# A retention block with a multiplicative FFN on one core: state products, weight conversion and copies in the head of the kernel put in another order

## The chip, the cores and the metric

The kernel runs on one core of a Trainium2 chip, with nothing on the other cores. The metric is the time of one execution on the device in microseconds (us), as the median over several executions. A core has five engines that work side by side, each with its own list of instructions which it takes strictly in order: TensorE (PE in the profile; its weight loads are shown apart as PEld), VectorE (DVE), ScalarE (ACT), GpSimd (POOL) and SyncE (SP), which here only issues transfers. An instruction waits until the engines and transfers it depends on have signalled.

## The reference, cut to what matters

```python
def _attn_ref(q, k, v):                      # 8 batches, 8 heads, 576 positions, 64 wide
    scores = scale * np.matmul(q, k.transpose(0, 1, 3, 2))
    gamma = 1.0 - 2.0 ** (-5.0 - np.arange(H))
    Dmat = np.where(rel >= 0, gamma[:, None, None] ** rel[None, :, :], 0.0)
    return np.matmul(scores * Dmat[None], v)

def _moe_ref(x, w1, w2, w3, w_out):          # x: 4608 tokens x 512
    a = x @ w1                               # 512 x 1024
    b = x @ w2
    h = a * b @ w3                           # 1024 x 1024
    return h @ w_out                         # 1024 x 512

# reference: x = attention out, (B,H,S,D) -> (B*S, H*D); out = _moe_ref(x, ...)
```

q, k and v are float32. The four weights are float64, and the kernel turns them into float32 itself, from their two 32-bit halves.

## The kernel before

**Attention by units.** The causal decay is split between the queries and the keys (the latter by scaling v), so that a sequence can be worked off in chunks with a running state. A unit `g` is a pair of batches and one of five chunks of positions (64, 128, 128, 128, 128). Unit `g` needs: its transfers (`load`); the scaling of q and of v by decay factors (`scale`, on GpSimd, VectorE or ScalarE as the call says); `front`, which transposes k and q on TensorE and copies them out of PSUM on ScalarE; `score`, the products of k and q on TensorE, masked by VectorE into `pm`; `state`, which adds k times v onto the running state in PSUM and copies it to `sb` for the next unit (ScalarE); and `pv`. `pv(g)` makes the unit's output in two PSUM banks: first the product of q with the state of the units before (L305, nothing for the first chunk), then `pm` times v (L312), and then ScalarE copies the banks into the token tiles `xT` (L317). Of the seven PSUM banks of the pool `acc`, all these products and those of the FFN take one each in turn.

**FFN by Strassen's scheme.** x @ w1 and x @ w2 are made with seven products in place of eight (`up(i, n, fp)`: 192 tokens of each of two batches, quarter `fp` of the columns). `up` needs sums of weights (`strassen_weights`, four VectorE operations L171, of which S2 is the second) and sums of tokens (`strassen_tokens`, L499). Its products follow each other on TensorE (L527): p1 (A11 B11), S2 T2, S3 T3, S1 T1, A22 T4, A12 B21, S4 B22. VectorE takes them into the tile `c` with adds (L532), ScalarE with copies (L540, L555), and L561 multiplies the two halves. S4 B22 is added onto the bank of S1 T1, and so waits for that product's add. w3 and w_out are multiplied with each other first (`w3_mm`), and the result is used in `down`.

**Weight conversion.** The weights come in blocks of 128 x 512 float64 (`load_block`, five raw buffers, so block n+5 can be loaded once block n is read). Blocks 0 to 3 are the first quarter of w1 and w2, 4 to 7 the second quarter, and so on. A block is converted by

- `begin_block`: three ScalarE steps for the exponent (L398 takes the top 16 bits without the sign, L399 turns them into the exponent's complement, L400 into the bits of a float), beside VectorE's L402 (top mantissa bits) and L405 (lower half added);
- `end_block`: VectorE's L416 (sign) and L429 (mantissa times power of two, into the weight tile). Behind that the next block to load is issued on SyncE's queue, and after the last block of a quarter come the four weight sums.

Both are written as a generator, `conversion()`, which stops after each step: L402 with the ScalarE steps is one, L405 one, L416 one, L429 one, the weight sums three. `convert(n)` runs the next n steps at the place where it is called, and `convert_up_to(n)` runs until n blocks are done. The list of numbers in L450 says behind how many converted blocks the next one is not begun ahead; otherwise a block is begun before the one in front of it is ended. `up` calls `convert` after each add (argument `conv`) and once after its first product, with a count taken from the list `owed`.

**The order.** No scheduler reorders: `manual_schedule` keeps every engine's list in the order of the program. The head of the kernel, L693 to L774, is written out by hand: units 0 to 4 with their transfers on SyncE's queue, the conversions between them, and the first five `up` calls. From L776 on loops take over.

Names used below: "unit 1" is the second unit (`g = 1`), "block 7" the eighth block. In the profile, `ld_q`, `ld_v` are the raw tiles, `tp` transposes, `kT`, `qT` their copies, `sc` scores, `st` the state in PSUM, `xps` the two output banks, `e` and `m` exponent and mantissa of a block, `wA` converted weights, `wS` weight sums, `T` token sums.

Of the kernel before, what the change touches and what calls it, by code (L numbers as in the profile page):

```python
# [42 lines left out]
def kernel(  # L43
# [202 lines left out]
    def score(g):  # L246
        c = g % NC
        sz = sizes[c]
        kT, qT = live["kT", g], live["qT", g]
        pm = pools["fr"].tile([P, 2, 2, NP, P], F32, tag="pm", name="pm", bufs=1)  # L250
        for b in range(2):
            sc = [acc.tile([P, NP, P], F32, tag="acc", name="sc") for j in range(2)]
            for p in range(NP):
                for j, hs in enumerate(heads):
                    nc.tensor.matmul(sc[j][:sz, p, :sz], kT[hs, b, p, :sz], qT[hs, b, p, :sz],  # L255
                                     start=True, stop=True)
            for j in range(2):
                nc.vector.tensor_mul(pm[:sz, b, j, :, :sz], sc[j][:sz, :, :sz],  # L258
                                     mask[:sz, :sz].unsqueeze(1).to_broadcast([sz, NP, sz]))
        live["pm", g] = pm  # L260

    def state(g):
        c = g % NC
        sz = sizes[c]
        if c == NC - 1:
            return
        vs = live["v", g]
        kn = live["k", g]
        if c == 0:
            live["st"] = st_ps.tile([P, 2, NP, D], F32, tag="st", name="st")  # L270
        st = live["st"]

        for b in range(2):
            for p in range(NP):
                for j, hs in enumerate(heads):
                    h = b * H + 2 * p + j
                    nc.tensor.matmul(st[hs, b, p, :], kn[:sz, h, :], vs[:sz, h, :],  # L277
                                     start=(c == 0 and b == 0 and p == 0), stop=(c == NC - 2),
                                     skip_group_check=True)
        sb = pools["fr"].tile([P, 2, NP, D], F32, tag="sb", name="sb")  # L280
        nc.scalar.copy(sb, st)
        live["sb", g + 1] = sb

    def pv(g):
        i, c = divmod(g, NC)
        sz = sizes[c]
        live["x", g] = True
        qT, vs, pm = live["qT", g], live["v", g], live["pm", g]

        parts = []  # L290
        for n in range(NB):
            lo, hi = max(starts[c], n * TB), min(starts[c] + sz, (n + 1) * TB)
            if lo < hi:
                m = i * NB + n
                if ("xT", m) not in live:
                    live["xT", m] = xps[m % 4 == 3].tile([P, NP, 2, TB], F32, tag="xT", name="xT")
                parts.append((live["xT", m], lo - n * TB, lo - starts[c], hi - lo))

        banks = [acc.tile([P, 2, 2, P], F32, tag="acc", name="xps") for r in range(2)]
        order = [(b, n) for b in range(2) for n in range(2)]  # L300
        if c > 0:
            for m, (b, n) in enumerate(order):
                for r, j in ((0, 0), (0, 1), (1, 0), (1, 1)):
                    p = 2 * r + n
                    nc.tensor.matmul(banks[r][heads[j ^ r], b, n, :sz], live["sb", g][heads[j], b, p, :],  # L305
                                     qT[heads[j], b, p, :sz], start=(m == 0), stop=False,
                                     skip_group_check=True)
        for m, (b, n) in enumerate(order):
            for r in range(2):
                for half in range(2):  # L310
                    p, j = 2 * r + n, half ^ r
                    nc.tensor.matmul(banks[r][heads[half], b, n, :sz], vs[:sz, b * H + 2 * p + j, :],  # L312
                                     pm[:sz, b, j, p, :sz], start=(c == 0 and m == 0), stop=True,
                                     skip_group_check=True)
        for x, to, fr, n in parts:
            for r in range(2):
                nc.scalar.copy(  # L317
                    x[:, 2 * r:2 * r + 2, :, to:to + n].rearrange("p n b s -> p b n s"),
                    banks[r][:, :, :, fr:fr + n])

# [60 lines left out]
    def begin_block():  # L383
        n = begun[0]
        t = live["raw", n]
        lo, hi = t[:, :, 0], t[:, :, 1]
        top = t.rearrange("p n t -> p (n t)").bitcast(BF16).rearrange("p (n u) -> p n u", u=4)[:, :, 3]
        e = raw.tile([P, CV], I32, tag="exp", name="e")
        m = raw.tile([P, CV], I32, tag="man", name="m")
        vec = nc.vector  # L390

        half = e.bitcast(BF16).rearrange("p (n u) -> p n u", u=2)[:, :, 1]
        func = mybir.ActivationFunctionType
        nc.scalar.activation(half, top, func.Abs)  # L398
        nc.scalar.activation(e, half.bitcast(U16), func.Relu, bias=lim[:, 0:1], scale=-1.0 / 16.0)  # L399
        nc.scalar.activation(e, e, func.Relu, bias=lim[:, 1:2], scale=-2.0 ** 23)  # L400

        vec.tensor_scalar(out=m, in0=hi, scalar1=0x000FFFFF, scalar2=0x00100000,  # L402
                          op0=ALU.bitwise_and, op1=ALU.bitwise_or)
        yield
        vec.scalar_tensor_tensor(m.bitcast(F32), in0=lo.bitcast(U32), scalar=2.0 ** -32, in1=m,  # L405
                                 op0=ALU.mult, op1=ALU.add)
        live["em", n] = e, m
        begun[0] += 1
        yield
# [34 lines left out]
    def conversion():  # L444

        yield from begin_block()
        while converted[0] < len(blocks):
            if begun[0] < len(blocks) and converted[0] not in (1, 2, 3, 7):  # L450
                yield from begin_block()
            yield from end_block()
            if begun[0] == converted[0] < len(blocks):
                yield from begin_block()
# [17 lines left out]
    def convert_up_to(n):  # L472
        while converted[0] < n:
            assert go_on() is None
# [231 lines left out]
    scale(0, "v")  # L706
    state(0)
    convert_up_to(1)
    pv(0)
    load(2, "kqv")  # L710
    load_block()
    load_block()
# [6 lines left out]
    convert(2)  # L719
    scale(1, "v")  # L720
    score(1)
    state(1)
    load(3, "kq")
    convert_up_to(3)
    convert(2)
    weight_sums = strassen_weights(0)
    next(weight_sums)
    pv(1)
    keep_busy(4)
    load(3, "v")  # L730
    load_block()
# [10 lines left out]
    convert(1)  # L742
    score(2)
    state(2)
    front(3, "k")
    scale(3, "q", True)
    load(4, "kq")
    convert(1)
    scale(3, "v", engine=nc.vector)
    convert(2)  # L750
    pv(2)
    front(3, "q")
    convert(2)
    load(4, "v")
    state(3)
    while ("S", 1) not in live:
# [3 lines left out]
    up(0, 0, 1, conv=2, tail=False)  # L760
    owed.append(2)
    front(4)
    pv(3)
    list(strassen_tokens(0, 1, nc.vector))
    score(4)
    aside.append(lambda: scale(4, "v", True))
    up(0, 1, 0, conv=2, tail=False)
    owed.append(2)
    pv(4)
    up(0, 1, 1, conv=[2, 1, 0, 2, 2], tail=False)  # L770
    owed.append(2)
    up(0, 0, 2, conv=[2, 1, 1, 2, 2], tail=False)
    owed.append(2)
    att_part.close()  # L774


# [92 lines left out]
    for g in range(NC, G):  # L869
        c = g % NC  # L870

        n = (1, 1, 1, 3, 1)[c] if g < 2 * NC else -(-len(todo) // (NC - c))
        if g + 2 < G and not in_blocks[g + 2]:
            load(g + 2, "k")
            load_blocks(g + 2, "q")
        if g + 1 < G:
            scale(g + 1, "v")
            if not in_blocks[g + 1]:
                front(g + 1, "k")
                front_blocks(g + 1, "q")  # L880
        half = (n + 1) // 2
        if in_blocks[g + 1]:
            scale_blocks(g + 1)

            work(n - 1)
            aside.extend(lambda nm=nm: front_blocks(g + 1, nm) for nm in "kq")
            work(1)
            while aside:
                aside.pop(0)()
            half = 0  # L890
        if in_blocks[g + 2]:
            load_blocks(g + 2, "q")
            load_blocks(g + 2, "k")
        work(half)
        pv(g)

        if g + 2 < G:
            queue = nc.scalar if in_blocks[g + 2] else nc.sync
            load(g + 2, "v", queue)
            if in_blocks[g + 2] and (g + 2) % NC != NC - 1:  # L900
                load(g + 2, "k", queue)
        if g + 1 < G:
            state(g + 1)
            score(g + 1)
        if g + 2 < G and not in_blocks[g + 2]:
            scale_blocks(g + 2)
        if g == NC + 1:
            list(strassen_tokens(1, 0))
            todo.extend((up, 1, 0, fp) for fp in range(NQ))
        if not (in_blocks[g + 1] and g + 1 < G):  # L910
            work(n // 2)
        if c == NC - 1:
            add_pair(g // NC)
# [45 lines left out]
```

## Time and profile before

| | us |
|---|---|
| median of four runs | 858.6 |
| lowest and highest run | 857.48, 859.38 |
| the profiled execution | 857.47 |
| its span, first to last instruction | 855.4 |

| stretch of the span, us | TensorE busy | VectorE busy | ScalarE busy | TensorE's clock | DMA, GB/s |
|---|---|---|---|---|---|
| 15.00 to 20.00 | 2.35 of 5.00 | 3.39 | 3.71 | 1.00 | 258 |
| 21.30 to 25.00 | 3.59 of 3.70 | 1.49 | 2.52 | 0.55 | 208 |
| 30.00 to 40.00 | 9.88 of 10.00 | 9.76 | 7.03 | 1.00 | 224 |
| 40.00 to 55.00 | 14.15 of 15.00 | 12.81 | 13.38 | 1.00 | 222 |
| 55.00 to 70.00 | 13.68 of 15.00 | 12.80 | 11.95 | 1.00 | 230 |
| 70.00 to 85.00 | 14.66 of 15.00 | 14.77 | 9.18 | 1.00 | 78 |
| 120.40 to 855.00 | 730.86 of 734.60 | 366.55 | 129.21 | 1.00 | 60 |

How to read it: the span is some 2 us shorter than the time of the same execution, since the time also holds what lies before the first and behind the last instruction. Busy time is the time in which at least one instruction of the engine ran in that stretch. The clock is the share of full speed that the chip granted to TensorE. In rows of the timeline, a number in brackets is the idle time of that engine just before the instruction, with what ended it. A row with a q behind the engine's name (SPq) is the issuing of a transfer.

### The profile page before, as it was taken

How to read it: one execution, taken by the hardware profiler on the slowest of the kernel's cores; microseconds unless marked ns; L12 is line 12 of the kernel's file. 1: busy time of each engine (PE TensorE's matmuls, PEld its weight loads, DVE VectorE, ACT ScalarE, POOL GpSimd, SP SyncE). 2: the span in 40 equal slices, each digit the busy share in tenths (PEclk: the TensorE clock that was granted, in tenths of full speed). 3: DMA queues.
4: the chain of work that ended last, by engine and by line, in shares of the span. 5: the costliest groups of instructions: out<-in, count | busy, mean ns of one | idle time of the engine just before them, and what ended most of it. 6: DMA issues, size and time to landing. Idle time of an engine off the chain costs nothing.

```text
span 855.4 us, 15413 instructions
## 1 busy us (share of the span) xinstructions
PE 842.9 (99%) x6289; PEld 770.0 (90%) x6289; DVE 466.5 (55%) x760; ACT 207.8 (24%) x390; POOL 111.8 (13%) x94
## 2 busy tenths in 40 slices
PE   7999999999999999999999999999999999999998
PEld 7989999644988999999999999999999999999996
DVE  4888999991644444454545544544454334334343
ACT  4786566670121112010211010111110201001000
POOL 1100010002112203220221130103030101000000
PEclk9999999999999999999999999999999999999999
DMA  9994464437056425352442161533140000000001
GB/s 192 222 221 121 76 149 124 125 97 111 7 115 117 88 38 96 65 94 48 83 91 38 28 119 32 93 76 50 33 67 26 2 25 1 25 26 1 25 1 49
DMA packets 214997, 63.99 MB, mean 75 GB/s; under 512 B 195848, under 2 KB 206344, under 8 KB 214928
## 3 DMA queue, kind: packets, MB, share of 16 engines
q1 hardware_dynamic: 168496, 43.33, 26.5%
q10 hardware_dynamic: 46432, 19.70, 10.2%
q8 instruction: 49, 0.80, 0.4%
q14 instruction: 20, 0.16, 0.1%
HBM read 53.55 MB, written 9.44 MB: 74 GB/s over the span
## 4 chain that ended last, share of the span: by engine, by line
PE 88%; DMA 4%; DVE 3%; ACT 2%; SPq 1%; issue 1%; POOL 0%; ACTq 0%; DVEq 0%
PE up L527 47%; PE po L642 25%; PE ps L480 6%; PE sc L255 3%; PE xps L312 3%; PE xps L305 2%; PE st L277 1%; DMA raw<-in_moe_w_dram 1%; DMA ld_v<-in_v_dram 1%; DMA ld_q<-in_q_dram 1%; SPq L115 1%; DVE c L532 1%; DVE pm L258 1%; DMA out_dram<-ot 0%; ACT kT L243 0%
## 5 line engine op out<-in xcount | busy, mean ns | idle before, releaser
L532 DVE TENSOR_TENSOR c<-up,c 128x384 f32<-128x384 f32 x240 | 132.6, 552 | 183.2 <-PE up L527 179.7
L527 PE MATMUL up<-xT,wA 128*128 128x192 f32 x1152 | 211.9, 327 | 0.0
L527 PEld LDWEIGHTS up<-xT,wA 128*128 128x128 f32 x1152 | 190.5, 190 | 2.6 <-issue 0.5
L527 PE MATMUL up<-T,wS 128*128 128x192 f32 x768 | 140.6, 326 | 1.7 <-DVE wS L171 1.5
L527 PEld LDWEIGHTS up<-T,wS 128*128 128x128 f32 x768 | 127.3, 190 | 2.2 <-issue 1.8
L642 PE MATMUL po<-w3o,ab 128*128 128x256 f32 x456 | 104.0, 380 | 0.2 <-ACT ot L664 0.2
L642 PEld LDWEIGHTS po<-w3o,ab 128*128 128x128 f32 x456 | 86.0, 190 | 12.0 <-ACT ot L664 0.6
L646 DVE TENSOR_TENSOR ot<-po,ot 128x256 f32<-128x256 f32 x90 | 38.0, 423 | 69.7 <-PE po L642 66.1
L555 ACT COPY c<-up 128x384 f32<-128x384 f32 x48 | 22.9, 476 | 216.8 <-PE up L527 216.8
L527 PE MATMUL up<-xT,wS 128*128 128x192 f32 x384 | 70.7, 327 | 1.5 <-DVE c L532 1.5
L258 DVE TENSOR_TENSOR pm<-sc,mask 128x512 f32<-128x512 f32 (+1 forms) x80 | 45.5, 628 | 46.3 <-PE sc L255 46.3
L527 PE MATMUL up<-T,wA 128*128 128x192 f32 x384 | 70.2, 326 | 0.0
L226 POOL TENSOR_TENSOR ld_v<-ld_v,gk 128x1024 f32<-128x1024 f32 (+1 forms) x18 | 35.0, 1947 | 266.1 <-DMA ld_v<-in_v_dram 253.6
L527 PEld LDWEIGHTS up<-xT,wS 128*128 128x128 f32 x384 | 63.5, 190 | 2.3 <-DVE c L532 2.1
L642 PE MATMUL po<-wB,forms 128*128 128x256 f32 x288 | 65.1, 379 | 0.0
L527 PEld LDWEIGHTS up<-T,wA 128*128 128x128 f32 x384 | 63.7, 190 | 0.0
L642 PEld LDWEIGHTS po<-wB,forms 128*128 128x128 f32 x288 | 54.7, 190 | 7.4
L480 PE MATMUL ps<-wo,w3T 128*128 128x512 f32 x128 | 55.1, 592 | 0.0
L540 ACT COPY c<-up 128x384 f32<-128x384 f32 x48 | 23.0, 479 | 129.5 <-PE up L527 75.5
L480 PEld LDWEIGHTS ps<-wo,w3T 128*128 128x128 f32 x128 | 24.3, 190 | 30.1 <-issue 29.4
L561 DVE TENSOR_TENSOR ab<-c 128x768 f32<-128x768 f32 x48 | 46.0, 959 | 4.3 <-ACT c L555 0.6
L499 POOL TENSOR_TENSOR T<-xT,T 128x384 f32<-128x384 f32 x20 | 20.5, 1030 | 162.9 <-PE up L527 162.2
(79 smaller groups left out, 820.0 us busy)
## 6 DMA issues: line engine op xcount, KB each, us to landing
raw<-in_moe_w_dram SPq DMA_DIRECT2D x72, 128.0 KB, 3.0
bl_q<-in_q_dram SPq DMA_DIRECT2D x208, 32.0 KB, 2.4
out_dram<-ot ACTq DMA_DIRECT2D x23, 256.0 KB, 2.1
bl_k<-in_k_dram SPq DMA_DIRECT2D x176, 32.0 KB, 2.3
ld_v<-in_v_dram ACTq DMA_DIRECT2D x10, 512.0 KB, 6.2
raw<-in_moe_w_dram SPq DMA_DIRECT2D x16, 256.0 KB, 6.3
raw<-in_moe_w_out_dram SPq DMA_DIRECT2D x32, 128.0 KB, 2.9
ld_k<-in_k_dram ACTq DMA_DIRECT2D x7, 512.0 KB, 8.8
```

Of the source, the lines that this page charges most:

```text
L226: engine.tensor_tensor(out=t, in0=t, in1=gam[:sz, c].unsqueeze(1).unsqueeze(3).to_broadcast([sz, 2, H, D]), op=ALU.mult)
L255: nc.tensor.matmul(sc[j][:sz, p, :sz], kT[hs, b, p, :sz], qT[hs, b, p, :sz], start=True, stop=True)
L258: nc.vector.tensor_mul(pm[:sz, b, j, :, :sz], sc[j][:sz, :, :sz], mask[:sz, :sz].unsqueeze(1).to_broadcast([sz, NP, sz]))
L312: nc.tensor.matmul(banks[r][heads[half], b, n, :sz], vs[:sz, b * H + 2 * p + j, :], pm[:sz, b, j, p, :sz], start=(c == 0 and m == 0), stop ...
L480: nc.tensor.matmul(ps, live["w3T", ft][:, g, :], live["wo"][:, g, :], start=(g == 0), stop=(g == KF - 1))
L527: nc.tensor.matmul(ps[:, w, :], a[:, w, r, :], b[:, r, :], start=(new and w == r == 0), stop=(w == r == 1), skip_group_check=True)
L532: nc.vector.tensor_add(c[:, to], ps, c[:, sb])
L540: nc.scalar.copy(c[:, 0], p1)
L555: nc.scalar.copy(c[:, 0], p1)
L561: nc.vector.tensor_mul(ab[:, 4 * fp:4 * fp + 4, :], c[:, :, 0, :], c[:, :, 1, :])
L642: nc.tensor.matmul(ps[nm], a[A][:, f, :], live["W"][B][:, f, :], start=(f == 0 and not on), stop=(f == NP - 1), skip_group_check=True)
L646: nc.vector.tensor_add(ot[:, to[0], to[1]], ps[nm], ot[:, sb[0], sb[1]])
```

## The change

1. `pv` is split. The product of q with the state becomes `pv_state(g)`, which `pv` calls itself if it has not run yet. `pv` no longer copies the banks out but returns a function that does. Everywhere but in two places the calls stay together, as `pv(g)()`.
2. For unit 1, `pv_state(1)` is called ahead of `state(1)`, and the conversion calls that followed `load(3, "kq")` move ahead of `state(1)` as well.
3. Block 7 is no longer begun before block 6 is ended (6 is added to the list of L450). For block 7 alone VectorE extracts the 11 bits of the exponent with two shifts in one instruction, and ScalarE's first two steps become one.
4. For units 2 and 3: the scaling of unit 3's q and the loads for unit 4 come ahead of the transposes of k of unit 3; three conversion steps in place of one come ahead of the scaling of unit 3's v; four in place of two behind `front(3, "q")`; the copies out of unit 2's banks come behind those.
5. One conversion step is added ahead of `pv(3)`, and one is taken from the last `owed` of the head.

```diff
+    def pv_state(g):
+        sz = sizes[g % NC]
+        qT = live["qT", g]
+        banks = live["xps", g] = [acc.tile([P, 2, 2, P], F32, tag="acc", name="xps") for r in range(2)]
+        if g % NC:
+            for m, (b, n) in enumerate(bank_order):
+                for r, j in ((0, 0), (0, 1), (1, 0), (1, 1)):
+                    p = 2 * r + n
+                    nc.tensor.matmul(banks[r][heads[j ^ r], b, n, :sz], live["sb", g][heads[j], b, p, :],
+                                     qT[heads[j], b, p, :sz], start=(m == 0), stop=False,
+                                     skip_group_check=True)
...
     def pv(g):
+        if ("xps", g) not in live:
+            pv_state(g)
...
-        for x, to, fr, n in parts:
-            for r in range(2):
-                nc.scalar.copy(
+        def evict():
+            for x, to, fr, n in parts:
+                for r in range(2):
+                    nc.scalar.copy(
...
+        return evict
...
-        nc.scalar.activation(half, top, func.Abs)
-        nc.scalar.activation(e, half.bitcast(U16), func.Relu, bias=lim[:, 0:1], scale=-1.0 / 16.0)
+        if n == 2 * NQ - 1:
+            vec.tensor_scalar(out=e, in0=hi, scalar1=1, scalar2=21,
+                              op0=ALU.logical_shift_left, op1=ALU.logical_shift_right)
+            nc.scalar.activation(e, e, func.Relu, bias=lim[:, 0:1], scale=-1.0)
+        else:
+            nc.scalar.activation(half, top, func.Abs)
+            nc.scalar.activation(e, half.bitcast(U16), func.Relu, bias=lim[:, 0:1], scale=-1.0 / 16.0)
...
-            if begun[0] < len(blocks) and converted[0] not in (1, 2, 3, 7):
+            if begun[0] < len(blocks) and converted[0] not in (1, 2, 3, 6, 7):
...
     score(1)
+    pv_state(1)
+    convert_up_to(3)
+    convert(2)
     state(1)
     load(3, "kq")
-    convert_up_to(3)
-    convert(2)
     weight_sums = strassen_weights(0)
     next(weight_sums)
-    pv(1)
+    pv(1)()
...
     state(2)
-    front(3, "k")
     scale(3, "q", True)
     load(4, "kq")
-    convert(1)
+    front(3, "k")
+    convert(3)
     scale(3, "v", engine=nc.vector)
-    convert(2)
-    pv(2)
+    copies = pv(2)
     front(3, "q")
-    convert(2)
+    convert(4)
+    copies()
...
     front(4)
-    pv(3)
+    convert(1)
+    pv(3)()
...
     up(0, 0, 2, conv=[2, 1, 1, 2, 2], tail=False)
-    owed.append(2)
+    owed.append(1)
```

As to the engines' lists: TensorE's differs only in that the 16 q-state products of unit 1 stand ahead of its 16 state products. VectorE's has one instruction more (the shift), ScalarE's one less. On SyncE's queue one transfer of block 10 moves ahead of that of unit 4's v. GpSimd's list is the same.

More of the change, by code (lines that the diff above doesn't have):

```diff
@@ L282, in state @@
         live["sb", g + 1] = sb
+    bank_order = [(b, n) for b in range(2) for n in range(2)]
+    def pv_state(g):
[9 more added lines that the diff above has]
+                                     skip_group_check=True)
     def pv(g):
+        if ("xps", g) not in live:
+            pv_state(g)
         i, c = divmod(g, NC)
@@ L287, in pv @@
         live["x", g] = True
-        qT, vs, pm = live["qT", g], live["v", g], live["pm", g]
+        vs, pm, banks = live["v", g], live["pm", g], live["xps", g]
         parts = []
@@ L297, in pv @@
                 parts.append((live["xT", m], lo - n * TB, lo - starts[c], hi - lo))
[L299 to L308, printed above, removed]
+        for m, (b, n) in enumerate(bank_order):
             for r in range(2):
@@ L314, in pv @@
                                      skip_group_check=True)
-        for x, to, fr, n in parts:
-            for r in range(2):
-                nc.scalar.copy(
-                    x[:, 2 * r:2 * r + 2, :, to:to + n].rearrange("p n b s -> p b n s"),
-                    banks[r][:, :, :, fr:fr + n])
+        def evict():
+            for x, to, fr, n in parts:
+                for r in range(2):
+                    nc.scalar.copy(
+                        x[:, 2 * r:2 * r + 2, :, to:to + n].rearrange("p n b s -> p b n s"),
+                        banks[r][:, :, :, fr:fr + n])
+        return evict
     blocks = [(("A", r, f), None) for f in range(2) for r in range(2)]
@@ L708 @@
     convert_up_to(1)
-    pv(0)
+    pv(0)()
     load(2, "kqv")
@@ L768 @@
     owed.append(2)
-    pv(4)
+    pv(4)()
     up(0, 1, 1, conv=[2, 1, 0, 2, 2], tail=False)
@@ L894 @@
         work(half)
-        pv(g)
+        pv(g)()
         if g + 2 < G:
```

## The prediction

> **What bounds the kernel now.** The page comes first. TensorE is busy nearly the whole span, and its share says where nothing can be won: after the head of the kernel there is almost no idle time left.
>
> ```profile
> span 855.4 us, 15413 instructions
> ...
> PE 842.9 (99%) x6289; PEld 770.0 (90%) x6289; DVE 466.5 (55%) x760; ACT 207.8 (24%) x390; POOL 111.8 (13%) x94
> ```
>
> So the second view is the list of what TensorE waited for (who, how long in total, how often, longest). It covers the whole span.
>
> ```profile
> PE tp L240 <- DVE ld_q L226: 2.7, 1, 2.7
> PE up L527 <- DVE wS L171: 1.5, 1, 1.5
> PE up L527 <- DVE c L532: 1.5, 2, 1.1
> PE sc L255 <- ACT qT L243: 1.2, 3, 0.6
> PE st L277 <- POOL ld_v L226: 0.2, 1, 0.2
> ```
>
> The 2.7 us (17.3 to 20.0) lies ahead of every edit. What the change can touch is the rest, and by the timeline the places are: 0.19 us at 24.9 (state of unit 1), 0.39 at 35.2 (weight load of S1T1), 0.63 at 41.5 (scores of unit 2), 1.53 at 54.8 (S2 of the second quarter), 0.26 at 69.0, 0.34 at 79.1 and 1.15 at 119.2 (both an add of L532). Together 4.5 us, the ceiling of any gain here. The large one that the edits surround is at 54.8, so the third view is VectorE's and then TensorE's timeline there (start, duration, instruction, idle time before it).
>
> ```profile
> 45.69 0.68 DVE L405 SCALAR_TENSOR_TENSOR m<-raw,m 128x512 f32<-128x512 uint32 x1
> 48.17 1.22 DVE L226 TENSOR_TENSOR ld_v<-ld_v,gk 128x1024 f32<-128x1024 f32 x1 [1.81 <-DMA ld_v<-in_v_dram]
> 49.32 0.68 DVE L416 SCALAR_TENSOR_TENSOR e<-raw,e 128x512 int32<-128x512 int32 x1
> 50.04 0.69 DVE L429 SCALAR_TENSOR_TENSOR wA<-m,e 128x512 f32<-128x512 f32 x1
> 50.76 0.43 DVE L402 TENSOR_SCALAR m<-raw 128x512 int32<-128x512 int32 x1
> 51.22 0.69 DVE L405 SCALAR_TENSOR_TENSOR m<-raw,m 128x512 f32<-128x512 uint32 x1
> ...
> 53.42 0.69 DVE L416 SCALAR_TENSOR_TENSOR e<-raw,e 128x512 int32<-128x512 int32 x1 [0.17 <-ACT e L400]
> ...
> 55.47 0.69 DVE L171 TENSOR_TENSOR wS<-wA 128x512 f32<-128x512 f32 x1
> ```
>
> ```profile
> 53.21 1.57 PE L527 MATMUL up<-xT,wA 128*128 128x192 f32 x8
> 56.31 0.89 PE L527 MATMUL up<-T,wS 128*128 128x192 f32 x4 [1.53 <-DVE wS L171]
> ```
>
> To see: VectorE idles 1.81 us for the v of unit 3 and then runs without a pause to S2 at 56.16; TensorE starts 0.15 later. That run holds blocks 5, 6 and 7 of the weights. Block 7 also needs three ScalarE steps (L398 to L400, 51.06 to 53.38).
>
> **The change, part by part.**
>
> *Unit 3's v scaled behind block 5's end.* L416 and L429 of block 5 go into the 1.81 us hole: 45.69 + 0.60 = 46.3, two instructions at a pitch of 0.72, done by 47.8, before the v lands at 48.1. The scale still starts at 48.17, so unit 3's state products (50.14) don't move. Free of cost; without the hole it would be 1.44.
>
> *Block 7's bits by VectorE.* New: one shift (two shifts in one instruction, line 413) ahead of L402. ScalarE loses L398 and keeps two of three steps. The nearest row for the shift is L402, also one integer source with two immediate operations: 0.43, pitch 0.46. The far end is L405's 0.69. I take 0.43: one source, same tile, same operand kinds.
>
> *The new order from 48.17*, by start-to-start pitches of the rows above: scale 48.17; block 6's L416 49.32 and L429 50.04; shift 50.76 to 51.19; L402 51.22; L405 51.68, free at 52.3. ScalarE's first kept step begins behind the shift at 51.22. Is ScalarE free? Its list now reads state copy 45.28, eight scalings of q (2.45, to 48.3), k copies (1.07, to 49.3), q copies 49.7 to 50.85 (TensorE's transposes end at 50.21), so yes. Two steps at 0.72 with a pitch of 0.75 end at 52.69. Then L416 52.72, L429 53.44, S3 54.05 (pitch 0.61), S2 54.77 to 55.46, and TensorE 0.15 later at 55.61 in place of 56.31: **0.70 gained**. The wait is 0.83 and not 0, since p1 of that `up` still ends at 54.78. With the shift at 0.69 ScalarE starts 0.26 later: 0.44.
>
> *Copies of unit 2's product moved behind block 7's steps on ScalarE*: 52.7 to 53.75 in place of 49.16 to 50.21. Queued behind them: the state copy of unit 3 (to 54.3) and L540's copy, which waits for p1 at 54.78 anyway. Two PSUM banks stay held, and the next users in the new order are the S2T2 and S3T3 products, at 55.6 or later. Cost nothing; past 55.6 it would be one for one. The k copies, moved behind the q scaling, come 2.4 later but TensorE needs them at 51.22 and has them at 49.3.
>
> *SyncE's queue.* Block 10's first transfer passes unit 4's v. They were issued at 54.39 and 53.75 and took 10.0 and 7.3 us, so they landed at 64.4 and 61.1; now about the other way round. The v is first touched at 77.49. Block 10 is needed by ScalarE at 64.85 less 0.70, or 64.15, so without this swap 0.3 would be lost there.
>
> *Start of the kernel (q-state product first, block 3 sooner).* Both rows are there: the product (1.10) is put into the 0.19 wait, so unit 1's product ends 0.17 sooner. Block 3's raw data have landed by 25.1 (last issue 21.24, 3.8 to landing), so its ScalarE steps can run from 25.1 to 27.4 instead of 26.76 to 29.06; the state copy comes behind them. But VectorE is busy without a pause from 24.92 to 36.0 either way, and the first token sum starts at 30.45 because VectorE is busy, not because of the copies (30.06). So the 0.17 is lost again at S1, which VectorE ends at 35.44: the 0.39 grows to 0.56. And 42.09 is set from outside: ScalarE waits 1.31 for block 4's data (35.73) and then runs to the q copy. **Gain 0**; bounds -0.2 and +0.2.
>
> *Conversions bunched in `up(0,1,0)`.* The third add (L532) sets the 0.34 at 79.1. Block 9's last step leaves the path (into the 1.54 us VectorE idles before 70.05), but a begin step comes in. From 74.58 the old order took 4.25 to that add (78.83). The new one is L402, L405, add, L416, L429, add, L402, L405, add: 0.46 + 0.60 + 0.47 + 0.72 + 0.60 + 0.47 + 0.46 + 0.60 = 4.38. **Cost 0.13.** Bounds: 0.34 gained if the add is early, 0.7 lost if one more L429 stands ahead. In the next `up` the add had 0.55 or more to spare. Unit 4's copies now stand behind three ScalarE steps (2.2 us) and come some 0.9 later; who waits is GpSimd's token sum, not needed by TensorE until after 120.
>
> *The 1.15 at 119.2* stays: VectorE's order there is unchanged, and its steps are slow (L405 1.38 and 1.02 against 0.69, L402 0.77 against 0.43) while GpSimd adds tokens, which TensorE's progress releases.
>
> **Sum.** 0.70 + 0 - 0.13 = 0.57. The profiled execution took 857.47, so 856.90 for it. It is the fastest of its kind: the four runs lie between 857.48 and 859.38 with a median of 858.6. On that median: **858.0**. Own range of this case 857.2 to 858.7.
>
> **A page against the row.** TensorE ran at half clock after the 2.7 us wait but not after the 1.53 (clock is the column after POOL):
>
> ```profile
> 21.30:24.60 3.30, 3.30 (x30) 3.30 (x32) 1.36 (x3) 2.52 (x4) 1.48 (x1) 0.50 0.76 199
> 54.78:56.31 1.53, 0.00 (x1) 0.03 (x1) 1.46 (x4) 1.47 (x3) 0.00 (x0) 1.00 1.02 181
> ```
>
> The Trainium skill ("TensorE: Matmul & The Clock Gate", "Part 1: The HAM clock gate") says the gate looks at free-running windows of about 3.4 us, so gaps below that should mostly be harmless, and the throttled stretch may fall differently from run to run. By the page nothing here would cost clock; by the row a gap of 2.7 did. I use the row.
>
> **Rivals.**
> *All of it (faster).* VectorE gets so far ahead that the waits at 54.8 and 79.1 vanish: 1.53 + 0.34 = 1.87, so 856.7; with the 1.15 as well 855.6. For it: the 1.81 hole is filled, and a begun block is one step further on in every later stage. Against: block 7's chain is serial from 50.76, and VectorE's order at 119 is the same.
> *Nothing (no change).* The 0.70 is won and given back: the shift slow (0.44), and the add at 79 later by half an L429 or so: 858.6. For it: the first wait already shows such a give-back.
> *The clock (slower).* Place: the same wait at 54.8. If the shift or its ScalarE steps come so late that S2 ends after 57.3, TensorE is idle for the 2.65 us after which the row shows the half clock. Price: 1.12 more wait and, from unit 1's scores (3.63 at half clock, 2.06 else), 1.57: 2.7, so 861.3. It decides when the shift starts after 52.6 instead of 50.76. Against: L402 started at 50.76 with no wait, so the data were there.
>
> **How the numbers follow.** Forecast 0.54, nothing 0.12, all of it 0.22, the clock 0.12. About 0.2% (1.7 us) is what a measurement of this kernel can tell from no change: below 856.9 or above 860.3. Faster: 0.22 from the second case and 0.03 of the forecast, 0.25. Slower 0.12. Within 0.63. The range 856.2 to 859.6 holds the forecast and nothing, and most of "all of it"; the clock is left out.
>
> **What would show it.** The wait before S2's product near 0.83, with the shift near 0.43 and ScalarE's step right behind it; block 5's end before 48; no wait for data at block 10; the wait at 79 near 0.47 and the one at 119 near 1.15; S1's weight load waiting some 0.56; TensorE at the scores of unit 2 still at 42.1. Wrong if TensorE's total wait falls by more than 1.7 us, or if a stretch past 54 shows a clock below 1.

## The result and the profile after

| | before | after |
|---|---|---|
| median, us | 857.57 (60 executions) | 856.48 (42 executions) |
| lowest and highest, us | 856.93, 859.38 | 855.17, 859.38 |
| ratio to before, 95% interval | | 0.9988 (0.9983 to 0.9992) |
| profiled execution, us | 857.47 | 857.26 |
| its span, us | 855.4 | 855.2 |

The change wins 0.12%, which is 1.03 us on the new median of before (0.69 to 1.46 us by the interval). The forecast was 0.57 us. The two profiled executions differ by only 0.21 us (that of after lies 0.78 above the median of its kernel), and that has to be understood before any other line of the two traces is compared.

The page of after, its first lines and the busy times:

```profile
span 855.2 us, 15409 instructions
...
PE 841.4 (98%) x6289; PEld 768.2 (90%) x6289; DVE 467.5 (55%) x761; ACT 207.3 (24%) x389; POOL 110.8 (13%) x94
```

VectorE has one instruction more and ScalarE one less, as the change says. What TensorE waited for in after (who, total us, times, longest):

```profile
PE tp L240 <- DVE ld_q L226: 2.3, 1, 2.3
PE sc L255 <- ACT qT L243: 2.0, 4, 1.2
PE st L277 <- POOL ld_v L226: 1.7, 1, 1.7
PE up L546 <- DVE c L551: 1.6, 2, 1.2
...
PE up L546 <- ACT c L559: 0.5, 1, 0.5
```

The 1.5 us wait on the weight sums is gone from the list, and a wait of 0.5 stands in its place. But the waits in the first 45 us are longer than in before. Those on ld_q and ld_v lie ahead of every edit: in this execution the first transfers landed later, and unit 2's scores began at 42.75 in place of 42.09. So 0.66 us was lost at the start before the order around S2 could win anything. It is luck as far as the profiles tell: over the nine profiles, this one and those below, that have the edit at the start, these scores begin anywhere from 41.60 to 43.12; in the two without it they begin at 42.09 (before) and 42.01 (no_start). The comparison that is free of that luck counts from the start of unit 2's scores (`sc`, the second row below) to the start of the S2 T2 product (the `T,wS` row), and from there to the scores of unit 5, far behind the last edit.

TensorE's timeline in after (start, duration, instruction, idle time before it):

```profile
42.75 2.06 PE L255 MATMUL sc<-qT,kT 64*128 64x128 f32 x32 [1.19 <-ACT qT L243]
...
53.86 1.57 PE L546 MATMUL up<-xT,wA 128*128 128x192 f32 x8
55.97 1.54 PE L546 MATMUL up<-T,wS 128*128 128x192 f32 x8 [0.54 <-ACT c L559]
```

From scores to S2 T2 it is 55.97 - 42.75 = 13.22 us; in before it was 56.31 - 42.09 = 14.22. **1.00 us is won here**, and the wait fell by as much, from 1.53 to 0.54. From S2 T2 to unit 5's scores it is 181.08 us against 180.94: **0.14 is given back**. The rest of the span agrees. 0.66 lost at the start, 1.00 won, 0.14 given back: 0.20 won, which is the difference of the two profiled executions (0.21). The 0.86 that the edits make by this count lies inside the interval of the ratio.

The profile names ScalarE's copy as what ended the 0.54. VectorE's list in after shows S2 (the second L171) ending at 55.13 + 0.69 = 55.82, the same 0.15 ahead of TensorE as in before. S2 is the real releaser; the copy ended at about the same time. In no_start below the copy ends at 55.21, behind the start of the product at 55.11, while S2 ends 0.15 ahead of it again.

```profile
46.94 0.68 DVE L435 SCALAR_TENSOR_TENSOR e<-raw,e 128x512 int32<-128x512 int32 x1
47.66 0.69 DVE L448 SCALAR_TENSOR_TENSOR wA<-m,e 128x512 f32<-128x512 f32 x1
48.64 1.22 DVE L226 TENSOR_TENSOR ld_v<-ld_v,gk 128x1024 f32<-128x1024 f32 x1 [0.29 <-DMA ld_v<-in_v_dram]
...
51.11 0.42 DVE L413 TENSOR_SCALAR e<-raw 128x512 int32<-128x512 int32 x1
51.45 0.42 DVE L421 TENSOR_SCALAR m<-raw 128x512 int32<-128x512 int32 x1
51.90 0.69 DVE L424 SCALAR_TENSOR_TENSOR m<-raw,m 128x512 f32<-128x512 uint32 x1
53.07 0.69 DVE L435 SCALAR_TENSOR_TENSOR e<-raw,e 128x512 int32<-128x512 int32 x1 [0.48 <-ACT e L419]
...
55.13 0.69 DVE L171 TENSOR_TENSOR wS<-wA 128x512 f32<-128x512 f32 x1
```

Block 5's end (46.94, 47.66) now stands in the hole ahead of the v, of which 0.29 us is left. Behind the v the list is block 6's end, the shift (L413), block 7's begin step and then 0.48 us of waiting for ScalarE's two steps (the line numbers of the conversion are 19 higher than in before).

ScalarE in after:

```profile
50.46 1.07 ACT L243 COPY qT<-tp 128x512 f32<-128x512 f32 x2 [0.65 <-PE tp L240]
51.57 0.72 ACT L415 ACTIVATE e<-e,lim 128x512 int32<-128x512 int32 x1
52.32 0.72 ACT L419 ACTIVATE e<-e,lim 128x512 int32<-128x512 int32 x1
```

L415 begins 0.04 behind the end of the shift (51.53).

### The profile page after: what moved, and what is told of

Same layout as the page of the kernel before. It is cut to its first block, busy times and chain, and to the rows that moved or that the text cites. A ratio compares the mean times of both kernels' runs of the same rounds, so it can differ in the third digit from the quotient of the medians.

```text
span 855.2 us, 15409 instructions
## 1 busy us (share of the span) xinstructions
PE 841.4 (98%) x6289; PEld 768.2 (90%) x6289; DVE 467.5 (55%) x761; ACT 207.3 (24%) x389; POOL 110.8 (13%) x94
## 4 chain that ended last, share of the span: by engine, by line
PE 93%; DVE 3%; DMA 2%; ACT 1%; issue 1%; SPq 0%; POOL 0%; ACTq 0%; DVEq 0%; POOLq 0%
PE up L546 49%; PE po L661 25%; PE ps L499 6%; PE sc L255 4%; PE xps L321 4%; PE xps L296 2%; PE st L277 2%; DMA ld_v<-in_v_dram 1%; PE tp L240 1%; DVE c L551 1%; DMA out_dram<-ot 1%; DMA raw<-in_moe_w_out_dram 0%; DVE wS L171 0%; DVE pm L258 0%; DVE e L435 0%
## 5 line engine op out<-in xcount | busy, mean ns | idle before, releaser
L551 DVE TENSOR_TENSOR c<-up,c 128x384 f32<-128x384 f32 x240 | 132.5, 552 | 183.2 <-PE up L546 178.7
```

The lines of the kernel that those rows point to most:

```text
L551: nc.vector.tensor_add(c[:, to], ps, c[:, sb])
```

## The experiments

All runs in one table. "Scores to S2 T2" is the interval above, "v" the start of the scaling of unit 3's v on VectorE counted from the start of unit 2's scores, "wait" the idle time of TensorE ahead of S2 T2, "rest" the time from S2 T2 to unit 5's scores. Each kernel was timed beside before; 0.001 of the ratio is 0.86 us.

| kernel | ratio to before, 95% | scores to S2 T2 | v | wait | rest |
|---|---|---|---|---|---|
| before | | 14.22 | 6.08 | 1.53 | 180.94 |
| after | 0.9988 (0.9983 to 0.9992) | 13.22 | 5.89 | 0.54 | 181.08 |
| no_shift | 0.9992 (0.9984 to 1.0001) | 13.91 | 5.86 | 1.23 | 181.10 |
| early_v | 1.0009 (1.0000 to 1.0018) | 14.55 | 5.89 | 1.87 | 181.11 |
| copies_at_once | 0.9987 (0.9978 to 0.9995) | 13.31 | 5.78 | 0.63 | 181.10 |
| no_start | 0.9987 (0.9978 to 0.9996) | 13.10 | 5.78 | 0.41 | 181.11 |
| start_only | 1.0000 (0.9992 to 1.0009) | 14.22 | 5.95 | 1.53 | 180.96 |
| no_step | 0.9982 (0.9973 to 0.9992) | 13.19 | 5.86 | 0.51 | 180.97 |
| v_first | 0.9991 (0.9982 to 0.9999) | 13.84 | 6.51 | 1.15 | 181.36 |
| light | 0.9970 (0.9958 to 0.9982) | 13.09 | 5.52 | 0.41 | 180.01 |
| light3 | 0.9972 (0.9960 to 0.9984) | 13.82 | 6.49 | 1.14 | 178.85 |

The intervals of the ratio are about 1.5 us wide, since the start differs from execution to execution, so single edits are told apart by the last columns, which come from one profile of each kernel. The rest repeats to 0.03 us in the five kernels that share the order behind S2 T2 (181.08 to 181.11). The interval up to S2 T2 does not repeat so well: it also moves with the start of the v, as v_first shows, so runs are compared at like starts.

### The shift undone (no_shift)

```diff
-        if n == 2 * NQ - 1:
+        if n < 0:
```

> The changed kernel with one edit undone: block 7's exponent comes from the three ScalarE steps again (the order of the blocks and all else stays). Measure: from the start of unit 2's scores to the start of S2 T2 on TensorE, 14.22 us in the profile of before, 13.22 in that of after. Theory (the gain is block 7's chain on ScalarE, which begins behind unit 3's q copies and hands its result to VectorE's last steps of block 7): three steps last 0.85 + 0.75 + 0.73 = 2.33 in place of 1.50, so the chain ends 0.86 later (the pitches of before: the last step ended 2.32 behind the start of the first), the interval is 14.08, the wait ahead of S2 T2 1.40, and 0.86 of the 1.0 us is lost: time 0.1 to 0.2 below before. Rival (the gain is VectorE's, from filling its hole at the v of unit 3, and the shift adds nothing): interval 13.2, time 1.0 below before. Rival (the 1.0 is an accident of the start of the profiled execution): the interval says nothing, and the time stays 1.0 below before or at it whatever the interval.

The interval is 13.91, so 0.69 of the 1.00 us is lost and the reading of block 7's chain holds. The 0.31 that stays is ScalarE's: its three steps begin 8.67 behind unit 2's scores, 0.30 sooner than in before (51.06 - 42.09 = 8.97), with its list in the new order. VectorE's row for the sign of block 7 shows who is late (0.48 in after):

```profile
53.20 0.69 DVE L435 SCALAR_TENSOR_TENSOR e<-raw,e 128x512 int32<-128x512 int32 x1 [1.53 <-ACT e L419]
```

The 0.17 that the expectation is off is a start of the first step that I had put too late: without a shift to wait for it began at 50.86, 8.67 behind unit 2's scores, in place of 8.82 in after. So in after the shift, and not the q copies, lets ScalarE begin.

### Unit 3's v scaled at its old place (early_v)

```diff
-    convert(3)
+    convert(1)
     scale(3, "v", engine=nc.vector)
+    convert(2)
```

> The changed kernel with one edit undone: unit 3's v is scaled one conversion step earlier in VectorE's list, ahead of block 5's last two instructions, as before the change. Theory: VectorE idles for the v again (about 1.8 us) and block 5's two instructions (0.72 + 0.61 = 1.33) come behind it, so the shift ends 1.33 later than unit 3's q copies and the whole of block 7's chain moves with it: interval from unit 2's scores to S2 T2 13.22 + 1.33 = 14.55, wait ahead of it about 1.9, 0.3 us slower than before. Rival (ScalarE alone sets block 7, VectorE's place for the v doesn't matter): 13.2, time 1.0 below before. Rival (half clock): with a wait of 1.9 the clock stays at 1.00 by the row of 1.53 us in before, and drops by the row of 2.7; then some 1.5 us more, time 1.5 or more above before.

14.55, the figure of the theory, and the time is on the slower side of before (0.8 us, 0 to 1.5). VectorE's and TensorE's rows, and the clock in the stretch (it is the column after POOL's time):

```profile
47.49 1.23 DVE L226 TENSOR_TENSOR ld_v<-ld_v,gk 128x1024 f32<-128x1024 f32 x1 [1.42 <-DMA ld_v<-in_v_dram]
...
51.30 0.42 DVE L413 TENSOR_SCALAR e<-raw 128x512 int32<-128x512 int32 x1
```

```profile
56.15 1.54 PE L546 MATMUL up<-T,wS 128*128 128x192 f32 x8 [1.87 <-DVE wS L171]
```

```profile
52.00:60.00 8.00, 6.13 (x47) 5.75 (x45) 7.38 (x13) 7.90 (x18) 0.00 (x0) 1.00 1.07 236
```

The hole is back, and the shift comes 51.30 - 41.60 = 9.70 behind unit 2's scores in place of 8.36. A wait of 1.87 us left the clock at 1.00. No_shift and early_v together say that neither edit carries the gain: all but the shift wins 0.31, all with the v at its old place loses 0.33, both together win 1.00. Block 7 begins behind block 6 now, which puts its bits later in VectorE's list; that this only pays when block 5 is out of the way is argued from the rows, since neither this edit nor the new place of the scaling of q was undone by itself.

### Unit 2's copies at once (copies_at_once)

```diff
-    copies = pv(2)
+    pv(2)()
...
-    copies()
```

> The changed kernel with one edit undone: the two copies out of unit 2's banks stand directly behind unit 2's product again, ahead of unit 3's q copies on ScalarE. The prediction put the move of these copies at nothing. Theory now: in after, the q copies and VectorE's shift end in the same instant (51.53), so what stands ahead of the q copies counts: the copies begin at 49.85, take 0.95, the q copies begin at 50.8 in place of 50.46, and block 7's first ScalarE step 0.33 later. Interval 13.55 in place of 13.22, wait 0.9, time 0.35 slower than after, 0.65 below before. Rival (as predicted, worth nothing): 13.2.

13.31: between the two, and the theory's 0.33 was too large. The copies fit partly into the 0.65 us for which ScalarE waits for the transposes anyway; block 7's first step began 8.87 behind unit 2's scores, 0.18 later than in no_start, whose v came equally early (5.78). Against that run the move is worth 0.2 us, against the profiled execution of after, where the shift was late, 0.1.

### The start: undone (no_start) and alone (start_only)

```diff
     score(1)
-    pv_state(1)
-    convert_up_to(3)
-    convert(2)
     state(1)
     load(3, "kq")
+    convert_up_to(3)
+    convert(2)
```

Start_only is the kernel before with the opposite edit.

> The changed kernel with the edit at the start undone: unit 1's state product first, then the product of q with the state, and block 3's ScalarE steps behind the copy of the state. Theory (the prediction: worth nothing, since unit 2's scores wait for block 4's data on ScalarE's list whatever TensorE does ahead): interval 13.2 as in after, the wait of the weight load of S1 T1 back to about 0.39 from 0.56, time 1.0 below before. Rival (the part of the gain that exceeds the forecast of 0.57 comes from the start): time only 0.6 below before.

> The kernel before with the edit at the start alone: q-state product of unit 1 ahead of its state products, block 3's steps ahead of them too. Theory (as predicted): unit 2's scores wait for block 4's data on ScalarE's list and the rest is as before: interval from unit 2's scores to S2 T2 14.2, time at before, within 0.3. Rival: this edit gives the 0.3 to 0.4 us by which the change beat the forecast: time 0.4 below before.

Undone, the whole gain stays; alone, nothing comes (the times say so to some 0.8 us, the intervals of 13.10 and 14.22 more closely). The predicted give-back is in the weight loads of S1 T1, of no_start and then of start_only:

```profile
35.75 1.27 PEld L546 LDWEIGHTS up<-T,wS 128*128 128x128 f32 x8 [0.39 <-PE up L546]
```

```profile
36.87 1.27 PEld L546 LDWEIGHTS up<-T,wS 128*128 128x128 f32 x8 [0.57 <-PE up L546]
```

What TensorE wins by the earlier product it waits at S1, 0.39 grown to 0.57.

Start_only shows one thing more, in VectorE's row for the sign of block 7:

```profile
54.45 0.69 DVE L435 SCALAR_TENSOR_TENSOR e<-raw,e 128x512 int32<-128x512 int32 x1 [0.31 <-ACT e L419]
```

Its v starts 0.13 sooner than in before, and the interval is the same 14.22: VectorE waits 0.31 for ScalarE's last step where it waited 0.17 in before. So in the old order ScalarE's chain, which begins 8.97 behind unit 2's scores in both, set S2, and an earlier VectorE alone would only have waited longer.

### The added step undone (no_step)

```diff
     front(4)
-    convert(1)
     pv(3)()
...
-    owed.append(1)
+    owed.append(2)
```

> The changed kernel without its last edit: no conversion step ahead of unit 3's product, two owed behind the head's last FFN call. Theory (the prediction: the step bunches VectorE's list and costs 0.13): wait at 79 back to 0.34 from 0.47, the one at 119 still 1.15, time 0.1 below the changed kernel, which is less than the runs can tell. Rival (the step is what lets later waits be short): a wait above 0.5 at 79 or a new one behind it, time 0.3 or more above the changed kernel.

The wait at 79 went back to 0.35 and the rest to 180.97: the step costs 0.11 to 0.14. The time is the lowest of the single edits, but its interval can't tell 0.1 us.

### Unit 4's v ahead of block 10 (v_first)

```diff
+    load(4, "v")
     convert(4)
     copies()
-    load(4, "v")
```

> The changed kernel with the transfer of unit 4's v issued ahead of block 10's first transfer again, as in before. Theory (the prediction: without the swap block 10 comes too late for ScalarE and VectorE): block 10's transfer, issued some 0.6 later and behind 512 KB, lands about 10.0 behind its issue (the row of before), at 65.9 in place of 62.5, where its first ScalarE step began at 64.5: a wait for data of about 1.4 there, some of it taken up by the idle 0.6 and 0.9 of VectorE behind it, unit 4's scores 0.3 to 0.9 later than 12.73 behind S2 T2, time 0.3 to 0.9 above the changed kernel. Rival (it lands in time, or the idle time takes all of it): 12.73, time as the changed kernel.

ScalarE's first step of block 10, and the scores of unit 4, in v_first:

```profile
64.48 0.80 ACT L417 ACTIVATE e<-raw 128x512 bf16<-128x512 bf16 x1 [2.22 <-DMA raw<-in_moe_w_dram]
```

```profile
68.67 2.06 PE L255 MATMUL sc<-qT,kT 64*128 64x128 f32 x32 [0.24 <-ACT qT L243]
```

ScalarE waits 2.22 us for the block, and unit 4's scores start 12.99 behind S2 T2 in place of 12.73: 0.26 lost. The swap that the change makes on SyncE's queue prevents that, and the prediction's 0.3 stands; the expectation's upper end (0.9) was too high.

This run's S2 T2 is late (13.84) for another reason. Its v of unit 3, issued ahead of the edit, was scaled 6.51 behind unit 2's scores. The table then gives a rule for the order of after: the interval is the v's start plus 7.33 (after, no_step, v_first and light3: 5.89, 5.86, 6.51 and 6.49 give 13.22, 13.19, 13.84 and 13.82), down to a floor of 13.1 that ScalarE's q copies set (no_start 5.78, light 5.52; in light the shift ends at 50.84, but ScalarE's step begins at 51.11, when the q copies let it, 8.67 behind the scores as in no_shift).

### The remaining waits: light and light3

```diff
-    up(0, 1, 0, conv=2, tail=False)
+    up(0, 1, 0, conv=[1, 1, 3, 3, 2], tail=False)
...
-            up(*todo.pop(0), conv=[1, 0, 1, 2, 2] if len(todo) == 5 else 2 if first else 1, tail=False)
-            owed.append(2 if first else 4)
+            up(*todo.pop(0), conv=[1, 0, 1, 2, 2] if len(todo) == 5 else [1, 1, 1, 1, 3] if len(todo) == 4 else 2 if first else 1, tail=False)
+            owed.append(2 if first or len(todo) == 5 else 4)
```

> The changed kernel with the conversion steps of two FFN calls dealt out otherwise, the same work in all: in the call that holds the wait at 79.2 (0.47), one step behind each of the first two adds and three behind each of the next two, in place of two behind each; in the call that holds the wait at 119 (1.15), one step behind each of the first four adds and three behind the fifth, with two in place of four behind its first product. Theory (both waits are only VectorE's list: steps that stand ahead of an add which TensorE needs for its bank): one instruction pair less (1.06 and 1.3 us) ahead of the third add, both waits go, 1.6 us faster than the changed kernel and about 2.6 below before. Rival (the steps are only put off): the waits appear at a later add or at the next call's weight sums, time as the changed kernel, 1.0 below before.

Both waits are gone, but one of 0.49 has come at the next call's third add:

```profile
127.44 1.57 PE L546 MATMUL up<-xT,wS 128*128 128x192 f32 x8 [0.49 <-DVE c L551]
```

So theory and rival each have a part: 1.07 of the 1.62 us is won (181.08 - 180.01), the rest is put off. Light3 takes one more step from ahead of that add:

```diff
-            owed.append(2 if first or len(todo) == 5 else 4)
+            owed.append(2 if first or len(todo) == 5 else 3 if len(todo) == 4 else 4)
```

> The kernel light with one more step put off: three steps in place of four are owed to the FFN call behind the one of 119, whose third add TensorE waited for at 127.44 (0.49). Theory (the deficit of VectorE is paid at whichever add comes first, and each step taken from ahead of it is worth its own 0.6 us until the wait is gone): the wait at 127.4 goes, and the 0.1 to 0.2 at 136.9 with it; from S2 T2 to unit 5's scores 179.4 us in place of 180.01, time 0.5 to 0.7 below light, about 3.1 below before. Rival (the step comes back as a wait where the product of w3 and w_out begins, at about 157): 180.0, time as light.

What TensorE waits for in light3 from 57 to 240 us, the whole list:

```profile
PE sc L255 <- ACT qT L243: 0.4, 1, 0.4
```

No add is waited for any more. The rest is 178.85, 1.16 below light and 2.23 below after, and the product of w3 and w_out starts without a wait. The expectation had 0.6: the later calls had each held a pause too short for the list of waits (the S4 B22 products at 146 and 155 took 1.57 in light, 1.46 in light3). Both kernels are faster than before by more than after is: 0.28% to 0.30%, 2.4 to 2.6 us, from five and six executions, with intervals of 0.18% to 0.42% and 0.16% to 0.40% against 0.08% to 0.17% for after. Which of the two is faster the times don't say: light3's profile has its v of unit 3 late by 0.97, which takes back 0.73.

## Why the prediction came out as it did

The direction, the size class and the mechanism were right; the median lies 1.5 us below the 858.0 named. Of that, 1.03 is the starting point: the four runs shown had a median of 858.6, sixty have 857.57, and the 857.47 taken for the fastest of its kind is about the middle. On the sixty the same sum gives 857.0. That was bad luck with four runs; it took the result to within 0.28 of the lower end of the range. The other 0.5 is a gain of 1.0 to 1.1 (by the ratio and by the medians) in place of 0.57, of which the trace explains 0.29 (0.86); the rest is within the interval.

- *Block 5's end in the hole, free*: confirmed. It ended at 48.35, which, counted from unit 2's scores, corresponds to 47.69 in before. Taking it out again costs the 1.33 of its two instructions (early_v).
- *Block 7's bits by VectorE and the new order, 0.70*: this is the mis-sized term; it measured **1.00**. The shift took 0.42 (0.43 assumed). From the v's start to TensorE the prediction had 55.61 - 48.17 = 7.44, the runs 7.33: the pitch from block 6's last instruction to the shift is 0.61, not the 0.72 read off the row of before. That is 0.11. The other 0.19 is when the v comes: 6.08 behind unit 2's scores in before, 5.89 in after. No edit accounts for it: with the same list ahead of it the v starts between 5.52 (light) and 6.51 (v_first), and its transfer took between 8.2 and 9.7 us from its issue over the eleven profiles. With the v of before the gain would have been 14.22 - (6.08 + 7.33) = 0.81. One reading under this term was off, too: VectorE did not run "without a pause" from the v to S2, its row at 53.42 has a wait of 0.17 for ScalarE, and by start_only it was that chain and not VectorE's list which set the old 14.22.
- *Copies moved behind block 7's steps, nothing*: the move costs nothing, but it also earns 0.1 to 0.2 (copies_at_once), which the prediction had not priced apart.
- *SyncE's queue, 0.3 prevented*: 0.26 (v_first).
- *The start, 0*: confirmed from both sides, with the give-back at S1 where it was named (0.57 against 0.56). That unit 2's scores would still begin at 42.1 was no test: over the eleven profiles they begin between 41.60 and 43.12.
- *Conversions bunched, 0.13*: 0.14 by the rest of the span, with the wait at 0.47, as named.
- *The 1.15 at 119 stays*: 1.15 again, though it wasn't a given: light removes it by dealing the same steps out otherwise.

Of the rivals, "all of it" asked for waits of zero at 54.8 and 79, which were 0.54 and 0.47. "Nothing" asked for a shift of 0.69 or a further L429 ahead of the add, neither of which is there. "The clock" was not reached: past 54 us after shows 1.00 throughout, early_v, where the wait grew to 1.87, still ran at 1.00, and 2.65 wasn't tried at this place.

The rows that confirm the last two points in after, both on TensorE:

```profile
79.22 1.57 PE L546 MATMUL up<-xT,wS 128*128 128x192 f32 x8 [0.47 <-DVE c L551]
...
120.17 1.57 PE L546 MATMUL up<-xT,wS 128*128 128x192 f32 x8 [1.15 <-DVE c L551]
```

## What to carry to other kernels

Where each execution starts a little differently, measure an edit between two events that enclose it, both on the bounding engine, and not by the span: here 0.66 us of luck at the start hid most of a gain of 0.86. A wait that is a chain of several engines has a floor from each of them, so edits that are worth 0.31 and -0.33 alone can be worth 1.00 together. Work that only has to be done some time belongs behind, not ahead of, the instruction that frees the bound engine's buffer: the same conversion steps, dealt out otherwise, won 2.23 us by the traces where all the reordering of the head won 0.86.

## What the hardware showed that was not expected

**VectorE's slow instructions follow GpSimd's, and not by line.** At 119 the prediction took L424 (L405 before) to be slow while GpSimd adds tokens. In light other instructions stand in that stretch, and of them those that begin while a GpSimd instruction runs are slow, but the adds that read PSUM are not. VectorE's and then GpSimd's timeline in light:

```profile
113.21 1.38 DVE L424 SCALAR_TENSOR_TENSOR m<-raw,m 128x512 f32<-128x512 uint32 x1
114.50 0.55 DVE L551 TENSOR_TENSOR c<-up,c 128x384 f32<-128x384 f32 x1
114.97 0.68 DVE L435 SCALAR_TENSOR_TENSOR e<-raw,e 128x512 int32<-128x512 int32 x1
...
116.04 1.02 DVE L448 SCALAR_TENSOR_TENSOR wo<-m,e 128x512 f32<-128x512 f32 x1
116.98 0.54 DVE L551 TENSOR_TENSOR c<-up,c 128x384 f32<-128x384 f32 x1
117.45 0.76 DVE L421 TENSOR_SCALAR m<-raw 128x512 int32<-128x512 int32 x1
```

```profile
112.78 1.25 POOL L518 TENSOR_TENSOR T<-xT 128x384 f32<-128x384 f32 x1 [26.10 <-issue]
115.39 2.52 POOL L518 TENSOR_TENSOR T<-xT,T 128x384 f32<-128x384 f32 x2 [1.36 <-PE up L546]
```

L448 takes 1.02 (0.69 elsewhere) and L421 0.76 (0.42), L551 (at 116.98) its usual 0.54, and L435, which begins between the two GpSimd rows, its usual 0.68, though the second one starts 0.26 us before it ends. After has such a pair as well, VectorE's row and then GpSimd's:

```profile
116.39 0.69 DVE L448 SCALAR_TENSOR_TENSOR wo<-m,e 128x512 f32<-128x512 f32 x1
```

```profile
116.57 2.53 POOL L518 TENSOR_TENSOR T<-xT,T 128x384 f32<-128x384 f32 x2 [1.36 <-PE up L546]
```

Here L448 begins 0.18 ahead of GpSimd and keeps its 0.69, though 0.51 us of it lie under that row (GpSimd's times are rough). So in these rows what runs when the VectorE instruction begins goes with the price, and not the overlap as such.

The Trainium skill ("SBUF — State Buffer", "Who interferes with whom") has it that VectorE instructions with two SBUF inputs contend with a GpSimd instruction that reads SBUF, and those in a two-port mode contend with GpSimd too, while one with at most one SBUF input outside those modes does not. The rows agree for L448 and L551, which takes its other operand from PSUM; L421 has one SBUF input, and whether it ran in such a mode no run here shows.

**The half clock at the start comes and goes.** The same stretch of the span in after and in no_step (clock in the column after POOL's time):

```profile
15.00:22.00 7.00, 6.81 (x68) 6.42 (x65) 4.86 (x8) 4.21 (x8) 0.00 (x0) 0.50 1.00 217
```

```profile
15.00:22.00 7.00, 6.80 (x64) 6.28 (x60) 4.70 (x7) 4.51 (x9) 0.00 (x0) 1.00 1.06 222
```

In before the half clock lay later, behind the wait of 2.7 us. In after TensorE had waited 2.3 and 1.7 us ahead of 15 us, in no_step 0.7 at most between 10 and 15. But the length of a wait doesn't settle it. No_shift, TensorE's row and the clock behind it, and then the same of no_start:

```profile
9.41 0.74 PE L240 MATMUL tp<-ident,ld_q 64*128 64x64 f32 x8 [1.05 <-DVE ld_q L226]
```

```profile
10.00:20.00 10.00, 9.19 (x114) 8.65 (x112) 6.54 (x12) 6.90 (x13) 1.90 (x1) 0.50 1.25 239
```

```profile
25.29 1.15 PE L277 MATMUL st<-ld_v,ld_k 128*64 128x64 f32 x32 [1.36 <-POOL ld_v L226]
```

```profile
25.00:30.00 5.00, 4.71 (x102) 4.30 (x103) 4.17 (x7) 3.45 (x6) 0.23 (x1) 1.00 1.30 227
```

A wait of 1.05 us stands ahead of ten us at half clock, one of 1.36 ahead of full clock, and 1.87 in early_v did no harm either. So the 2.65 us at which the prediction set its third rival is one case and not a limit. What decides it was not tried.
